# Memory updates moved behind PV as 32-column matmuls, maxima transposed by VectorE, a finer head

## The chip, the cores and the metric

The kernel runs on one core of a Trainium2 chip. The metric is the device time of one execution in microseconds (us); the median of three runs before the change is 1011.85 us. A core has five engines with a queue each, executed in order: TensorE (PE in the profile, its weight loads as PEld), VectorE (DVE), ScalarE (ACT), GpSimd (POOL) and SyncE (SP, which issues all DMAs here). They meet through semaphores.

## What is computed

Two attention branches, A and B, over the same x (2048 tokens of 640 features, 32 heads of 20), mixed per token by a gate. Each branch goes through four segments of 512 tokens and carries a memory `M`, `z` per head:

```python
def _A_ref(x, wq, wk, wv, wo, beta):
    # q, k, v: x @ w, split into 32 heads and 4 segments of 512 tokens
    phi = lambda t: jnp.where(t > 0, t + 1.0, jnp.exp(t))
    for s in range(4):
        qs, ks, vs = q[:, :, s], k[:, :, s], v[:, :, s]
        logits = jnp.einsum("bhqd,bhkd->bhqk", qs, ks) * scale + mask
        a_dot = jnp.einsum("bhqk,bhkd->bhqd", _softmax(logits), vs)
        pq = phi(qs)
        num = jnp.einsum("bhld,bhde->bhle", pq, M)
        den = jnp.einsum("bhld,bhd->bhl", pq, z)[..., None] + 1e-6
        outs.append(g * num / den + (1.0 - g) * a_dot)      # g = sigmoid(beta)
        pk = phi(ks)
        M = M + jnp.einsum("bhld,bhle->bhde", pk, vs)
        z = z + jnp.einsum("bhld->bhd", pk)
    return o @ wo                                            # o: outs put together

g = _sigmoid((x * gate_w).sum(-1, keepdims=True))
return g * A(x) + (1 - g) * B(x)
```

The mask lets a query see keys up to its own position in the segment.

## The kernel before

The work is cut into eight windows t = 2 x segment + branch. Features are tiled in five blocks m of 128 (a block touches 7 or 8 heads), tokens in four blocks n of 128. The projections run at full precision as three products of high and low parts (`wh`, `wl` of the weights, rows `hi`, `lo` of x). High and low parts of q and k go to DRAM (`qd`, `kd`) and come back by groups of four heads, a "quad" i = 8t + u, into `qst[i % 4]`, `kst[i % 4]`, with two heads on partitions 0 to 63 and two on 64 to 127.

Each quad then takes these steps:

- S units (`s_unit`, L1236 on PE): scores with queries on the partitions. DVE takes the row maxima (L1223) into `mx`.
- The maxima are split in high and low (`m_unit`, `mt`, one tile of 128 x 32), transposed and written into the spare rows of `qst` by two DMAs. Before the change the transpose is `mrow_unit`: two turns on PE (L1261), a cast on ACT to `mr` (L1278).
- T units (`t_unit`, L1326): scores again with keys on the partitions, the maximum subtracted by those rows, exp on ACT, the triangle cut by POOL.
- PV (`pv_unit`, L1346): the sums over keys, four heads side by side, each with 32 columns of weights from `vst` (v and a column of ones, 21 columns a head), over all 128 rows of the array.

The memory of a branch is `mbds[t % 2][m]`: for each feature of block m, its sums with the 21 columns of each head the block touches. `got_pk` turns phi(k) to tokens on partitions (`back_unit`, into the row `pkn`), `update_unit` (L987) multiplies it with `vst`, DVE copies the sum out, and POOL clears what belongs to other heads and adds (`keep_own_heads`, L369, L373, L1008). Windows 0 to 5 do this, five updates each. The memory after window t is read by `mem_unit` (L905) of window t + 2, which runs per token block for a lower and an upper group of heads.

Nearly all of this runs as two streams on PE: one uses the array's upper 64 rows, one the lower, and a "unit" has first a part on one half and then on the other. PV and the head use all rows at once. The order of everything is set by a planner in the kernel: it advances a clock with assumed durations, keeps the pools of SBUF rows (`big`, 35), PSUM banks (8) and weight buffers (`wst`, 3), starts queued work by priority, and has a table `RULES` with, for each quad, the order of S and T units and seven numbers (pacing, lag, room and waits). `later` puts a unit in a list that the streams draw from. `lat=` in `dma` is the time the planner assumes until a transfer has landed. The chip itself follows only the queues and semaphores that come out.

The head (`job_head`, L841) is the first two projections, while x and the first weights land. `warm_up` runs nine products of zeros ahead of it (L349), and `IDLE_STEPS` puts seven more between its steps. `head_gates` makes the sigmoids of beta (L619, L620).

## Time and profile before

| | before |
|---|---|
| three runs | 1010.74, 1011.85, 1012.91 us |
| span of the profiled execution, first to last instruction | 1010.0 us |
| granted TensorE clock | 1.000 |
| PE / PEld busy | 99% / 85% |
| DVE / ACT / POOL busy | 74% / 66% / 60% |
| DMA | 236.42 MB, mean 234 GB/s |

The profiled execution shows its span, 1010.0 us; the fastest run is 0.7 us above that and the median 1.85 us, which is the time around the instructions. Groups give the number of instructions, busy time, the mean length of one and the engine's idle time before them with what ended it; matmuls overlap, so that mean is longer than the time an instruction keeps its half of the array. A full fp32 matmul is one row of the program's order and two instructions (passes) in the profile. In a timeline, rows are start, length, engine and line, and the bracket is the idle time before.

### The profile page before, as it was taken

What the parts mean: (1) busy time and instruction counts of PE and PEld (TensorE: products, weight loads), DVE (VectorE), ACT (ScalarE), POOL (GpSimd) and SP (SyncE); (2) the same over time, 40 slices, a digit from 0 to 9 for tenths busy, and PEclk for the clock granted to TensorE, in tenths of its full rate; (3) what the DMA queues carried; (4) which work ended last, traced back from release to release, by engine and by line L of the source; (5) the groups of instructions that cost most, each with busy time, mean ns of one, the idle gap of its engine ahead of it and who ended that gap; (6) DMA issues with size and microseconds to landing.
All of it is one profiled execution on the core that took longest, in us unless ns stands there. A gap on an engine that the chain in (4) does not pass through costs nothing.

```text
span 1010.0 us, 30764 instructions
## 1 busy us (share of the span) xinstructions
PE 998.5 (99%) x11262; PEld 857.8 (85%) x11262; DVE 751.3 (74%) x2562; ACT 666.4 (66%) x1371; POOL 602.4 (60%) x1039
## 2 busy tenths in 40 slices
PE   9999999999999999999999999999999999999998
PEld 7998888978898888888889988888888897889776
DVE  4577677857897777786778857778676887789854
ACT  5476767767766677676676557766666575675682
POOL 4555657755575655666656466576675566556561
PEclk9999999999999999999999999999999999999999
DMA  7997879969796877896679677788666978658521
GB/s 241 282 313 238 284 249 317 296 197 280 241 307 211 268 224 213 255 274 204 180 227 289 196 230 229 215 273 277 200 198 201 304 235 248 201 190 269 155 89 63
DMA packets 146449, 236.42 MB, mean 234 GB/s; under 512 B 12950, under 2 KB 45883, under 8 KB 145979
## 3 DMA queue, kind: packets, MB, share of 16 engines
q1 hardware_dynamic: 146298, 234.46, 75.5%
q8 instruction: 89, 1.46, 0.6%
q14 instruction: 62, 0.50, 0.2%
HBM read 145.26 MB, written 94.65 MB: 238 GB/s over the span
## 4 chain that ended last, share of the span: by engine, by line
PE 91%; DMA 5%; DVE 2%; ACT 1%; issue 1%; SPq 0%; POOL 0%; DVEq 0%; ACTq 0%; POOLq 0%
PE bank L795 53%; PE bank L1346 14%; PE bank L1326 7%; PE bank L1236 7%; PE bank L905 3%; PE bank L987 3%; PE bank L947 2%; DMA wst<-in_a_wv_dram 1%; DMA row<-rowg 1%; PE bank L1261 1%; DMA qd<-row 1%; DMA row<-in_xT_dram 1%; DVE row L1411 1%; DMA dots<-row 1%; PE bank L1165 0%
## 5 line engine op out<-in xcount | busy, mean ns | idle before, releaser
L1223 DVE CUSTOM_DVE_ANT_0 bank<-bank,tri 128x256 f32<-128x256 f32 (+3 forms) x1024 | 474.5, 519 | 163.0 <-PE bank L1236 125.0
L795 PE MATMUL bank<-row,wh 64*128 64x512 f32 x2308 | 513.2, 402 | 0.0
L1318 ACT ACTIVATE p<-bank 128x512 f32<-128x512 f32 x548 | 301.5, 600 | 115.2 <-PE bank L1326 91.8
L795 PEld LDWEIGHTS bank<-row,wh 64*128 64x128 f32 x2308 | 329.1, 185 | 10.1 <-issue 0.2
L1319 POOL TENSOR_SCALAR_AFFINE_SELECT p<-p 128x256 f32<-128x256 f32 (+1 forms) x548 | 205.1, 382 | 200.6 <-ACT p L1318 187.1
L795 PE MATMUL bank<-row,wl 64*128 64x512 f32 x1154 | 312.5, 399 | 0.0
L549 POOL TENSOR_TENSOR wl<-wst,wh 128x640 fp32r<-128x640 f32 x115 | 180.1, 1569 | 72.7 <-ACT wh L547 69.5
L795 PE MATMUL bank<-wvh,row 64*128 64x320 f32 (+1 forms) x1280 | 191.0, 313 | 0.0
L795 PEld LDWEIGHTS bank<-row,wl 64*128 64x128 f32 x1154 | 182.9, 185 | 3.8
L1236 PE MATMUL bank<-kst,qst 60*128 60x384 f32 (+3 forms) x1024 | 177.1, 317 | 3.5 <-ACT mr L1278 2.0
L1326 PE MATMUL bank<-qst,kst 62*128 62x128 f32 (+3 forms) x1024 | 175.9, 317 | 1.3 <-DVE mx L1223 1.3
L795 PEld LDWEIGHTS bank<-wvh,row 64*128 64x128 f32 x1280 | 160.0, 185 | 2.1 <-issue 0.4
L1223 DVE DVE_READ_ACCUMULATOR2_ANT mx<- 128x1 f32 x1024 | 143.8, 140 | 0.0
L1346 PE MATMUL bank<-p,vst 128*32 128x384 f32 (+3 forms) x1836 | 141.4, 423 | 0.0
L1236 PEld LDWEIGHTS bank<-kst,qst 60*128 60x128 f32 x1024 | 132.6, 186 | 9.5 <-ACT mr L1278 2.8
L1326 PEld LDWEIGHTS bank<-qst,kst 62*128 62x128 f32 x1024 | 130.7, 186 | 6.8 <-DVE mx L1223 2.4
L1346 PEld LDWEIGHTS bank<-p,vst 128*32 128x32 f32 x1836 | 57.4, 110 | 80.9 <-issue 58.2
L795 PE MATMUL bank<-wvl,row 64*128 64x320 f32 (+1 forms) x640 | 109.1, 312 | 0.0
L547 ACT CAST wh<-wst 128x640 fp32r<-128x640 f32 x119 | 86.7, 740 | 25.1 <-PE bank L795 17.7
L795 PEld LDWEIGHTS bank<-wvl,row 64*128 64x128 f32 x640 | 87.0, 186 | 0.4 <-issue 0.2
L1376 ACT COPY row<-bank 128x512 f32<-128x512 f32 x58 | 34.2, 590 | 69.8 <-PE bank L1346 64.9
L524 POOL TENSOR_TENSOR wvl<-wst,wvh 128x640 fp32r<-128x640 f32 (+1 forms) x48 | 60.1, 1258 | 31.9 <-ACT wvh L521 30.9
(121 smaller groups left out, 1223.4 us busy)
## 6 DMA issues: line engine op xcount, KB each, us to landing
qst<-qd SPq DMA_DIRECT2D x128, 240.0 KB
kst<-kd SPq DMA_DIRECT2D x128, 240.0 KB
qd<-row SPq DMA_DIRECT2D x40, 512.0 KB
kd<-row SPq DMA_DIRECT2D x40, 512.0 KB
dots<-row SPq DMA_DIRECT2D x56, 256.0 KB
wst<-wmix SPq DMA_DIRECT2D x35, 320.0 KB
row<-dots SPq DMA_DIRECT2D x42, 256.0 KB
qd<-row SPq DMA_DIRECT2D x40, 256.0 KB
```

Source lines behind the costliest of these rows:

```text
L524: put("G", 0.77 * n, lambda: nc.gpsimd.tensor_tensor(out=wl[:, a:b, :VN], in0=w3, in1=r32(wh[:, a:b, :VN]), op=ALU.subtract), end, prio=4)
L547: put("A", 0.625, lambda: nc.scalar.copy(wh, w3), lambda: put(lo_eng, lo_cost, lambda: lo.tensor_tensor(out=wl, in0=w3, in1=r32(wh), op=AL ...
L549: lambda: lo.tensor_tensor(out=wl, in0=w3, in1=r32(wh), op=ALU.subtract), end, prio=3), prio=6)
L795: return nc.tensor.matmul(bank_of, lhsT=w[ROWS[half]], rhs=x_[ROWS[half]], start=start, stop=stop)
L905: return nc.tensor.matmul(pm[:, a - h0:c - h0, :].rearrange("p h e -> p (h e)"), lhsT=r32(pqTs[t, m][ROWS[half], P * n:P * (n + 1)]), rhs= ...
L1223: put("D", w / 960.0 + 0.105, lambda: nc.vector.tensor_tensor_reduce(out=sc[:, off:off + w], in0=sc[:, off:off + w], in1=tri[:, L - w:], s ...
L1236: lane_ops[half].append((mm(w), lambda pair=pair, qb=qb, off=off, w=w, r=r, sc=sc: nc.tensor.matmul(sc[:, off:off + w], lhsT=q[r, pair, P ...
L1318: put("A", 0.483, lambda: nc.scalar.activation(pt, sc, AF.Exp, scale=SCALE), lambda: (bank.give(sc), put("G", 0.15 + 0.105 * len(todo), la ...
L1319: "G", 0.15 + 0.105 * len(todo), lambda: nc.gpsimd.affine_select(out=blocks, in_=blocks, pattern=[[0, len(todo)], [1, P]], base=0, channel ...
L1326: lane_ops[half].append((mm(w), lambda pair=pair, kb=kb, off=off, w=w, r=r, sc=sc: nc.tensor.matmul(sc[:, off:off + w], lhsT=k[r, pair, P ...
L1346: nc.tensor.matmul(po[32 * j:32 * j + 32, P * kb:], lhsT=vst[t % 2][:, kb, h * E1:h * E1 + 32], rhs=pts[i, n, f][0][:, off:off + w], start ...
L1376: either(0.483, lambda: nc.scalar.copy(r32(oT), po), 0.605, lambda: nc.vector.tensor_copy(r32(oT), po), end, 2)
```

## The change

Six things change together.

1. `update_unit` goes. An update now waits in `upd_due` until the next PV, behind whose matmuls up to three run (`updates`), with 32 features as weights over all 128 rows and only the 2 or 3 heads these touch as columns. One update is 16 matmuls in four column groups instead of 8 matmuls on halves. The result is copied by four DVE copies of 32 partitions; memory and `mt` tiles are zeroed at the start, since each copy writes only its window. The v products of window t + 2 wait for the update's matmuls, not for the whole update.
2. `mrow_unit` goes: DVE transposes the maxima, four blocks of 32 x 32 (`turn_rows`), straight into `mr`.
3. The head runs single products as soon as their parts are there; the seven idle steps go. x of the first segment is staged through four rows, and weights beyond the first two are asked for once the first x tile has been split.
4. Memory units are split at head 16 instead of 19.
5. The planner assumes longer landing times for wv (1.2 to 2.6), later x (1.2 to 3.0) and the gate rows and denominators (1.2 to 2.2).
6. `RULES` is another table, with an entry for every quad.

```diff
-        0: "STTSTSSTST 1.010 2.38 0.25 8 0.0 1.6 1",
...
+        0: "TSTSTSTSTS 1.01 2.38 0.23 8 0 1.6 1",
+        1: "SSTSTSTSTT 1.01 2.38 0.34 8 1.4 1.6 1",
...
-    IDLE_STEPS = {3: 5, 4: 2}
...
+        for t in (*mbds[0], *mbds[1], *mt_store.free):
+            nc.gpsimd.memset(t, 0.0)
...
-        if i >= len(jobs) or i in staged:
+        if i >= len(jobs) or i in staged or i >= len(HEAD0) and not x_begun:
...
-                dma(0.53 * n, lambda: nc.sync.dma_start(out=w3, in_=src[m // 4][:, a:b, :]), landed, prio=need[i], lat=1.2)
+                dma(0.53 * n, lambda: nc.sync.dma_start(out=w3, in_=src[m // 4][:, a:b, :]), landed, prio=need[i], lat=2.6)
...
+    x_first = Store([])
+    x_first_rows, x_begun = [], []
...
+                x_hi[s, k] = (hi, lo)
...
+                if s:
+                    big.give(st)
+                    return
+                x_first.give(st, *([x_first_rows[-1]] if k == 0 else []))
+                if k == 0:
+                    x_begun.append(1)
+                    for i in range(len(HEAD0), 9):
+                        stage(i)
+                if k == KT - 1:
+                    big.give(*x_first_rows)
...
-                out=r32(st), in_=xT[P * k:P * (k + 1), L * s:L * (s + 1)]), landed, prio=need[job_index[2 * s, "q", 0]] - 4 * (s > 0), lat=1.2 if s else 1.1)
-
-        big.want((F32R, F32R, F32), got, prio=4, spare=SPARE if s else 0)
+                out=r32(st), in_=xT[P * k:P * (k + 1), L * s:L * (s + 1)]), landed, prio=need[job_index[2 * s, "q", 0]] - 4 * (s > 0), lat=3.0 if s else 1.1)
+
+        if s:
+            big.want((F32R, F32R, F32), got, prio=4, spare=SPARE)
+        else:
+            x_first.want(1, lambda st: big.want((F32R, F32R), lambda hi, lo: got(hi, lo, st), prio=4))
...
-        todo = [(k, i) for k in range(KT) for i in range(len(HEAD0))]
+        todo = [(k, i, j) for k in range(KT) for i in range(len(HEAD0)) for j in range(3)]
         pps, n = {}, {}
+
+        def there(x):
+            k, i, j = x
+            return i in (split if j == 1 else split_hi_) and (0, k) in (xs if j == 2 else x_hi)
+
         while todo:
-            ready_ = [x for x in todo if x[1] in split and (0, x[0]) in xs]
-            if not ready_:
+            x = next((x for x in todo if there(x)), None)
+            if x is None:
                 blocked[0] = "head"
                 yield None
                 continue
-            k, i = ready_[0]
-            todo.remove((k, i))
+            todo.remove(x)
+            k, i, j = x
             if i not in pps:
                 pps[i], n[i] = bank.free.pop(0), 0
-            (wh, wl), (xh, xl) = split[i], xs[0, k]
-            for w, x_ in ((wh, xh), (wl, xh), (wh, xl)):
-                whole(STEP, lambda: nc.tensor.matmul(
-                    pps[i], lhsT=w[:, k, :], rhs=x_, start=(n[i] == 0), stop=(n[i] == 3 * KT - 1)))
-                n[i] += 1
-
-                for _ in range(IDLE_STEPS.get(sum(n.values()), 0)):
-                    idle_step()
-                yield STEP
+            w, o = split_hi_[i][j == 1], x_hi[0, k][j == 2]
+            whole(STEP, lambda: nc.tensor.matmul(
+                pps[i], lhsT=w[:, k, :], rhs=o, start=(n[i] == 0), stop=(n[i] == 3 * KT - 1)))
+            n[i] += 1
+            yield STEP
...
-        h0, h1 = ((0, 19), (19, 32))[h]
+        h0, h1 = ((0, 16), (16, 32))[h]
...
-                later(3, 1.0, lambda: ok(), lambda: update_unit(t, m, pkn), False)
+                upd_due.append((t, m, pkn, ok))
...
-    def update_unit(t, m, pkn):
+    upd_due = deque()
+    upd_run = set()
+    UPD = 63 / 1200.0 + 0.0027
+
+    def windows(m):
+        for j in range(4):
+            f0 = P * m + 32 * j
+            a, c = f0 // DH, (f0 + 31) // DH + 1
+            yield slice(32 * j, 32 * j + 32), a, c
+
+    def updates():
+        todo = [x for x in upd_due if x[3]()][:3]
+        if not todo or not bank.free:
+            return
+        b = bank.free.pop(0)
+        off = 0
+        done = then_all(len(todo), lambda: bank.give(b))
+        for x in todo:
+            upd_due.remove(x)
+            t, m, pkn, _ = x
+            nh = HI[m] - LO[m] + 1
+            v = b[:, off:off + nh * E1].rearrange("p (h e) -> p h e", e=E1)
+            off += nh * E1
+            for n in range(NB):
+                for r, a, c in windows(m):
+                    nc.tensor.matmul(
+                        v[r, a - LO[m]:c - LO[m], :].rearrange("p h e -> p (h e)"),
+                        lhsT=r32(pkn[:, P * n + r.start:P * n + r.stop]), rhs=vst[t % 2][:, n, a * E1:c * E1],
+                        start=(n == 0), stop=(n == NB - 1), skip_group_check=True,
+                    )
+            now[0] += 8 * UPD
+            upd_run.add((t, m))
+            after_whole(lambda t=t, m=m, pkn=pkn, v=v: updated(t, m, pkn, v, done))
+        advance(now[0])
+
+    def updated(t, m, pkn, v, done):
         s = t // 2
-        mbd = mbds[t % 2]
+        mbd = mbds[t % 2][m]
         nh = HI[m] - LO[m] + 1
-        b = bank.free.pop(0)
-
-        def run(half, n, start, stop):
-            return nc.tensor.matmul(
-                b[:, :nh * E1], lhsT=r32(pkn[ROWS[half], P * n:P * (n + 1)]),
-                rhs=vst[t % 2][ROWS[half], n, LO[m] * E1:(HI[m] + 1) * E1],
-                start=start, stop=stop,
-            )
-
-        ops = [[(quad4(nh * E1), lambda a, z, half=half, n=n: run(half, n, a, z)) for n in range(NB)] for half in range(2)]
-        v = b[:, :nh * E1].rearrange("p (h e) -> p h e", e=E1)
 
         def end():
             upd_done.add((t, m))
 
...
-        return split_unit(*ops, take)
+        def take(dst):
+            for r, a, c in windows(m):
+                h = slice(a - LO[m], c - LO[m])
+                nc.vector.tensor_copy(dst[r, h, :], v[r, h, :])
+
+        def got(tmp):
+            def add():
+                keep_own_heads(tmp[:, :nh, :], m)
+                nc.gpsimd.tensor_tensor(out=mbd, in0=mbd, in1=tmp[:, :nh, :], op=ALU.add)
+
+            put("D", 0.44, lambda: take(tmp), lambda: (
+                done(), put("G", 1.34, add, lambda: (mt_store.give(tmp), end()), prio=2)), prio=3)
+
+        big.give(pkn)
+        if s == 0:
+            put("D", 0.44, lambda: take(mbd), lambda: (
+                done(), put("G", 0.8, lambda: keep_own_heads(mbd, m), end, prio=2)), prio=3)
+        else:
+            mt_store.want(1, got)
...
-        yield from hold_on(lambda: t < 2 or oTs_begun[t - 2] == 8 and all((t - 2, m) in upd_done for m in range(KT)), "v")
+        yield from hold_on(lambda: t < 2 or oTs_begun[t - 2] == 8 and all((t - 2, m) in upd_run for m in range(KT)), "v")
...
     def m_ready(i):
         m_done.add(i)
-        later(0, 0.2, lambda: True, lambda: mrow_unit(i))
-
-    def mrow_unit(i):
+        mr_store.want(1, lambda mr: put("D", 0.4, lambda: turn_rows(i, mr), lambda: send_rows(i, mr), prio=1), prio=0)
+
+    def turn_rows(i, mr):
+        mt = mts.pop(i).rearrange("p f c n -> p (f c n)")
+        for j in range(NB):
+            nc.vector.transpose(r32(mr[:, 32 * j:32 * j + 32]), r32(mt[32 * j:32 * j + 32, :]))
+
+    def send_rows(i, mr):
         t, u, q, k = quad(i)
-        mt = mts.pop(i)
-        b = bank.free.pop(0)
-        mtf = r32(mt.rearrange("p f c n -> p (f c n)"))
-        ops = [[(TURN, lambda a, z, r=r: nc.tensor.transpose(b[:32, r], mtf[r], ident[r, r]))] for r in ROWS]
-
...
-            put("A", 0.15, lambda: nc.scalar.copy(mr, b[:32, :P]), send, prio=1)
-
-        return split_unit(*ops, lambda: mr_store.want(1, got))
+
+        def sent():
+            mr_done.add(i)
+            mr_store.give(mr)
+
+        done = then_all(2, sent)
+        for half in range(2):
+            r = 64 * half + 60
+            dma(0.3, lambda half=half, r=r: nc.sync.dma_start(
+                out=r32(q[r:r + 2, :, :].rearrange("p a (b n) -> p (a b) n", b=NB)),
+                in_=r32(mr[16 * half:16 * half + 16, :]),
+            ), done, prio=-2, some=True, issue=0.68)
...
             advance(now[0])
+        updates()
         now[0] += 0.11
...
-            out=r32(d), in_=lanes_of(t)[:, DH:DH + 1, :].to_broadcast([H, 4, L])), landed, prio=-1, lat=1.2)
+            out=r32(d), in_=lanes_of(t)[:, DH:DH + 1, :].to_broadcast([H, 4, L])), landed, prio=-1, lat=2.2)
...
-    put("G", 1.6, ones_tiles, prio=1)
+    put("G", 2.8, ones_tiles, prio=1)
+    big.want((F32,) * 4, lambda *rows: (x_first_rows.extend(rows), x_first.give(*rows[:3])))
     for k in range(KT):
         if k < len(HEAD0):
             stage(k)
         want_x(0, k)
-    for i in range(len(HEAD0), 9):
-        stage(i)
```

Three places show how the order moves. First PE in window 0, where the update of one feature block stands (`bank<-vst,row`); before, the rows of an update lie between those of the projections:

```order
L795 MATMUL bank_139<-row_25_199,wh_145 128x512
L795 MATMUL bank_137<-row_15_193,wh_147 128x512
L795 MATMUL bank_139<-row_30_202,wh_145 128x512
L795 MATMUL bank_137<-row_20_196,wh_147 128x512
L987 MATMUL bank_135<-vst_88,row_229_369 128x147
L795 MATMUL bank_137<-row_25_199,wh_147 128x512
L987 MATMUL bank_135<-vst_88,row_229_369 128x147
L795 MATMUL bank_139<-row_7_189,wh_145 128x512
L987 MATMUL bank_135<-vst_88,row_229_369 128x147
L1236 MATMUL bank_134<-kst_84,qst_80 128x512
```

and after, behind the last block of PV (L1392) of quad 0:

```order
L1392 MATMUL bank_137<-p_890_998,vst_88 32x256
L1392 MATMUL bank_137<-p_781_915,vst_88 32x128
L1392 MATMUL bank_137<-p_782_916,vst_88 32x128
L1392 MATMUL bank_137<-p_843_966,vst_88 32x128
L1392 MATMUL bank_137<-p_844_967,vst_88 32x128
L1031 MATMUL bank_136<-vst_88,row_223_369 32x42
L1031 MATMUL bank_136<-vst_88,row_223_369 32x63
L1031 MATMUL bank_136<-vst_88,row_223_369 32x42
```

The eight half-height rows of 147 columns have left the two streams, and the update stands in one piece behind PV, 42 and 63 columns wide.

Second, the maxima of quad 0 (`mt`). Before, PE turns them between projections:

```order
L987 MATMUL bank_140<-vst_88,row_351_551 128x147
L795 MATMUL bank_138<-row_19_195,wh_151 128x512
L678 MATMUL bank_134<-ident,gate 32x64
L1261 MATMUL bank_141<-ident,mt_676 32x64
L795 MATMUL bank_136<-row_7_189,wh_149 128x512
L795 MATMUL bank_138<-row_24_198,wh_151 128x512
L795 MATMUL bank_136<-row_14_192,wh_149 128x512
```

and after, DVE turns them between the maxima (L1275, where "ISA" is the custom maximum and its read-out into `mx`) of later quads and the low parts of projections (L786):

```order
L1275 ISA bank_135,mx_545<-bank_135,tri 128x128
L1275 ISA mx_545 128x1
L645 TENSOR_SCALAR gate<-gate 128x4 x2
L1311 STREAM_TRANSPOSE mr_160<-mt_668 32x32 x4
L786 TENSOR_TENSOR row_514_695<-bank_139,row_513_694 128x512
L1275 ISA bank_140,mx_716<-bank_140,tri 128x512
L1275 ISA mx_716 128x1
L786 TENSOR_TENSOR row_520_701<-bank_136,row_519_700 128x512
L1275 ISA bank_134,mx_716<-bank_134,tri 128x512
```

The turn has left PE and stands on DVE, four transposes in a row.

Third, ACT in the head. Before, the high parts of x (`row<-row`) follow each other, and the sigmoids of beta (`gmem`, `gdot`, `gcol`) come behind them and two weights:

```order
L592 CAST row_14_192<-row_16_194 128x512
L592 CAST row_19_195<-row_21_197 128x512
L592 CAST row_24_198<-row_26_200 128x512
L592 CAST row_29_201<-row_31_203 128x512
L547 CAST wh_149<-wst_144 128x640
L547 CAST wh_151<-wst_142 128x640
L521 CAST wvh<-wst_143 128x2x320
L619 ACTIVATE gmem_92<-beta_204 128x32
L619 ACTIVATE gdot_94<-beta_204 128x32
```

and after:

```order
L604 CAST row_20_195<-row_5_189 128x512
L604 CAST row_25_197<-row_6_190 128x512
L644 ACTIVATE gmem_92<-beta_199 128x32
L644 ACTIVATE gdot_94<-beta_199 128x32
L644 ACTIVATE gcol_132<-gcol_132 128x1
L644 ACTIVATE gmem_93<-beta_200 128x32
L644 ACTIVATE gdot_95<-beta_200 128x32
L644 ACTIVATE gcol_133<-gcol_133 128x1
L604 CAST row_72_233<-row_4_188 128x512
L604 CAST row_77_236<-row_7_191 128x512
```

The six activations on beta now stand between the third and the fourth x tile.

42 lines of the change are left out of this document (8 added, 34 removed), and 122 rows, old and new, of the table RULES.

## The prediction

> **What bounds the kernel now.** I read the page's busy table and its chain first, then the waits of TensorE, then the groups kept apart by shape, then the timeline at the places the change touches.
>
> ```profile
> span 1010.0 us, 30764 instructions
> PE 998.5 (99%) x11262; PEld 857.8 (85%) x11262; DVE 751.3 (74%) x2562; ACT 666.4 (66%) x1371; POOL 602.4 (60%) x1039
> PE 91%; DMA 5%; DVE 2%; ACT 1%; issue 1%; SPq 0%; POOL 0%; DVEq 0%; ACTq 0%; POOLq 0%
> ...
> PE bank L1236 <- ACT mr L1278: 2.0, 2, 1.5
> ...
> PE bank L1326 <- DVE mx L1223: 1.3, 1, 1.3
> ...
> PE bank L947 <- DVE row L751: 0.4, 1, 0.4
> ...
> PEld bank L1346 <- issue: 63.5, 256, 0.4
> PEld bank L1261 <- issue: 7.3, 37, 0.2
> ```
>
> PE busy at 99% alone would prove little, since matmul ends are modelled. The waits prove more: the six rows of the matmul queue's waits for other engines, first and last shown, sum to 6.7 us (1.5 of them at the very start), the chain is 91% PE, and most work runs as two independent streams, one on each half of the array's rows. So a microsecond of array time that is removed is a microsecond of span, as long as the other engines keep up. An instruction on one half counts half. The few real stalls come from in-order queues:
>
> ```profile
> 218.20 0.72 ACT L521 CAST wvh<-wst 128x640 fp32r<-128x640 f32 x1 [2.16 <-DMA wst<-in_a_wv_dram]
> 218.83 0.25 ACT L1278 CAST mr<-bank 32x128 fp32r<-32x128 f32 x1
> 219.13 0.50 PE L1236 MATMUL bank<-kst,qst 60*128 60x512 f32 x1 [1.45 <-ACT mr L1278]
> ...
> 423.43 0.44 PE L1326 MATMUL bank<-qst,kst 62*128 62x384 f32 x2 [1.34 <-DVE mx L1223]
> ...
> L1406 DVE SCALAR_TENSOR_TENSOR row<-row,gcol,row 128x512 f32<-128x512 f32 x7 | 7.6, 1079 | 6.4 <-DMA row<-rowg 6.3
> ```
>
> ACT stands 2.16 us in front of a weight that has not landed, the small `mr` cast is queued behind it, and PE loses 1.45 us. At 423 us the same happens on DVE behind the gate rows (L1406).
>
> **The updates.** The trace has 480 passes of L987 (a full fp32 matmul is two), 240 on each half.
>
> ```profile
> L987 PE MATMUL bank<-vst,row 64*128 64x147 f32 x384 | 50.0, 288 | 0.0
> L987 PE MATMUL bank<-vst,row 64*128 64x168 f32 x96 | 17.9, 310 | 0.0
> ...
> 212.22 0.28 PE L987 MATMUL bank<-vst,row 64*128 64x147 f32 x1
> 212.34 0.41 PE L987 MATMUL bank<-vst,row 64*128 64x147 f32 x2
> ```
>
> One pass lasts 0.28 us and two in a row 0.41, so a 147-column pass occupies its half for 0.125-0.13 us (0.125 from here on), a 168-column one by ratio 0.143. Removed: (384 x 0.125 + 96 x 0.143) / 2 = 30.9 us of the array.
>
> What comes instead, 16 matmuls per update with 32-column weights over all 128 rows, has one relative in the trace, PV:
>
> ```profile
> L1346 PE MATMUL bank<-p,vst 128*32 128x256 f32 x512 | 39.4, 379 | 0.0
> L1346 PE MATMUL bank<-p,vst 128*32 128x128 f32 x484 | 25.2, 273 | 0.0
> L1346 PEld LDWEIGHTS bank<-p,vst 128*32 128x32 f32 x1836 | 57.4, 110 | 80.9 <-issue 58.2
> ...
> 68.14 2.36 PE L1346 MATMUL bank<-p,vst 128*32 128x512 f32 x32
> ...
> 68.13 0.16 PEld L1346 LDWEIGHTS bank<-p,vst 128*32 128x32 f32 x8 [0.19 <-issue]
> 68.59 0.13 PEld L1346 LDWEIGHTS bank<-p,vst 128*32 128x32 f32 x4 [0.30 <-issue]
> ```
>
> Four column groups stream side by side. 128 columns more cost 379 - 273 = 106 ns, 0.83 ns a column. A window of 32 features touches 2 or 3 heads, 42 or 63 columns, so by streaming a pass of the four groups takes 63 x 0.83 + 3 = 0.055 us; an update is 4 blocks x 2 passes = 8 of them, 0.44 us, and 30 updates 13.2 us. The bounds: if the 42-column groups set the pace (0.035), 8.4 us; if each pass had to wait out a whole load (0.110 us), 26.4 us. No row has a stream this short, and PV's last block (128 columns, 106 ns) is as long as its load, so it cannot decide. I take 13.2, because eight loads of 0.11 us fit in 0.16 us: they start 7 ns apart, so the loads of four groups overlap instead of queueing, and four are issued at 68.59 while the stream before them runs on. Net -17.7 us (between -4.5 and -22.5). The drain of the array around PV is paid already, since the updates sit directly behind it.
>
> [...]
>
> Each update also waits for the next PV (64 in 1010 us, so up to 16 us) holding one of 35 SBUF rows. Nobody reads the memory before the window two steps on; I cost that at nothing, and if rows run short the T units wait.
>
> **The maxima.** 128 transposes on PE (L1261) and 64 ACT casts go; 256 transposes of 32x32 come to DVE.
>
> ```profile
> 213.97 0.40 PE L795 MATMUL bank<-row,wh 64*128 64x512 f32 x1
> ...
> 214.71 0.22 PE L1261 MATMUL bank<-ident,mt 64*32 64x64 f32 x1
> 214.74 0.47 PE L795 MATMUL bank<-row,wl 64*128 64x512 f32 x1
> ...
> L921 DVE RECIPROCAL mw<-mw 128x13 f32<-128x13 f32 x24 | 5.8, 241 | 0.8
> L919 DVE SCALAR_TENSOR_TENSOR mw<-bank,gq 128x13 f32<-128x13 f32 x24 | 4.0, 165 | 2.1 <-PE bank L905 2.1
> L1010 DVE COPY mt<-bank 128x147 f32<-128x147 f32 x16 | 4.7, 302 | 3.1 <-PE bank L987 3.1
> ...
> 275.00:400.00 125.00, 125.00 (x1443) 109.05 (x1440) 100.10 (x327) 82.42 (x168) 78.70 (x135) 1.00 0.80 245
> ```
>
> A turn takes 0.03 us of its half, and the product behind it starts some 0.08 late (0.47 against 0.40), since its weights cannot load earlier: 0.11 us. In 37 of 128 cases (the issue waits above) a turn comes straight behind PV, where the array is refilling anyway; those are free. (128 - 37) x 0.11 / 2 = -5.0 us (between 0 and -7).
>
> DVE has no such transpose in the trace. By its smallest operations it costs 0.165 to 0.241 us, 42 to 62 us for 256. The copies of an update become four of 32 partitions: 120 x 0.165-0.3 less 30 x 0.302, 11 to 27 us more. DVE goes from 751 to some 805-840 us of 984, and in its densest stretch, 275 to 400 us (third busy figure of that row), from 100 in 125 to about 109 in 122. It has room, but queues lengthen: I add 2.5 us of PE waits, 0.04 us for each of the 64 quads (between 0 and 12). ACT loses 64 x 0.25 us, worth nothing.
>
> **Memory units.** Split at 16, the lower unit needs one matmul less per token block:
>
> ```profile
> L905 PE MATMUL bank<-mbd,row 64*128 64x21 f32 x48 | 8.1, 247 | 0.0
> ...
> 697.68 4.81 PE L905 MATMUL bank<-mbd,row 64*128 64x84 f32 x74
> ```
>
> 74 passes in 4.81 us over both halves are 0.062 each whatever their width, so 48 fewer are -3.0 us (0 to -3).
>
> **The head.**
>
> ```profile
> 1.52 4.21 PE L349 MATMUL bank<-qst 128*128 128x512 f32 x9 [1.52 <-DVE qst L353]
> ...
> 5.52 0.78 PE L841 MATMUL bank<-row,wh 128*128 128x512 f32 x1
> 6.69 1.31 PE L349 MATMUL bank<-qst 128*128 128x512 f32 x5
> ...
> 8.29 2.70 ACT L592 CAST row<-row 128x512 fp32r<-128x512 f32 x4 [1.78 <-DMA row<-in_xT_dram]
> ...
> 13.48 0.23 ACT L619 ACTIVATE gmem<-beta 128x32 f32<-128x32 f32 x1
> ...
> 14.70 0.39 PE L841 MATMUL bank<-row,wh 128*128 128x512 f32 x1
> ...
> 16.17 0.20 ACT L619 ACTIVATE gcol<-gcol 128x1 f32<-128x1 f32 x1 [0.35 <-DVE gcol L626]
> ```
>
> 30 steps of about 0.23 us are 7.0, but the head runs from 5.52 to 14.9, so 2.4 us are fillers and waiting for x. Fewer transfers in flight and finer steps should recover that. Against it, the six beta activations, which took 13.48 to 16.37 with DVE in between, now stand on ACT ahead of the last two x casts, and x tile 3 is sent only when tile 0's row is free. I take -1.2 (0 to -2.4). Without fillers PE may idle about 1 us at a time. The rows of L349 show full rate by then: five in 1.31 us, where the first nine took 4.21. [...]
>
> **The assumed landing times** (wv, x, gate rows) are raised, which moves the instruction that stalled at 218 us behind other work. PE's waits behind such places are the 6.7 us above less the 1.5 at the start, about 5; I take -3.5 (0 to -5). The new table of rules may move as much either way.
>
> **Sum.** -17.7 - 5.0 - 3.0 - 1.2 - 3.5 + 2.5 = -27.9 us, a span of 982.1 against 1010.0. The median of the runs, 1011.85, is 1.85 above that span; with the same offset, 984.
>
> **Rivals.**
> 1. The short passes are paced by their loads: 26.4 instead of 13.2, so 997. For it: no stream under 106 ns in the trace. Against it: the loads 7 ns apart. 11%.
> 2. Loads do not overlap at all: 0.055 + 0.110 a pass, 30 x 8 x 0.165 = 39.6 us, more than the 30.9 removed, so 984 + 26.4 = 1010, no change. PV's 2.36 us speaks against it. 3%.
> 3. DVE becomes the bound: it must come out slower if more than 28 us of the 53-89 us added to DVE surface on PE, 0.44 us a quad. The stall at 423 us shows the path (maxima late, S units keep their banks, PE waits); against it stand DVE's 259 idle us, 4 a quad. It would give about 1015. 4%.
> 4. The other stalls go too, another 8 us: 976. 14%.
>
> The forecast as told, 977 to 991, has 68%. The range from 973 to 997 takes in rivals 1 and 4 in the main and leaves out 2 and 3. By the three runs (1010.74 to 1012.91) a change under 0.2%, 2 us, cannot be told from none: faster 0.93, same 0.03, slower 0.04.
>
> **What would show it.** Right: L987 and L1261 gone; the 32 short matmul passes behind a PV within about 0.45 us; turns on DVE under 0.25 us; the waits of PE on ACT `mr` gone; the head ending near 13.7 us; DVE near 82%. Wrong: updates near 0.9 us each; PE waiting for DVE's maxima or transposes; T units waiting for SBUF rows.

## The result and the profile after

| | before | after |
|---|---|---|
| median of the runs shown together | 1011.45 us (1010.74 to 1012.91) | 997.84 us (997.83 to 999.21) |
| span of the profiled execution | 1010.0 us | 996.1 us |

The ratio is 0.9875, with a 95% interval from 0.9856 to 0.9894. The forecast was 984 with a range from 973 to 997: the direction was right, the gain was half of what was told (13.6 us instead of 27.9), and the time lies just above the range.

First the page of the changed kernel: span, busy times, and the shares of the chain.

```profile
span 996.1 us, 31535 instructions
...
PE 979.4 (98%) x11559; PEld 821.2 (82%) x11559; DVE 814.0 (82%) x2904; ACT 654.4 (66%) x1310; POOL 604.5 (61%) x1052
...
PE 84%; DVE 7%; DMA 4%; issue 2%; POOL 2%; SPq 1%; ACT 1%; DVEq 0%; ACTq 0%; POOLq 0%
```

PE is as busy as before, and DVE is at the 82% that was forecast. The chain has changed: DVE carried 2% of it, some 20 us, and now carries 7%, some 70 us. PE's share fell from 91% to 84%. Something on DVE now ends last.

The new work, in the groups kept apart by shape (line 1031 is the updates, 1052 their copies, 1311 the turned maxima):

```profile
L1311 DVE STREAM_TRANSPOSE mr<-mt 32x32 f32<-32x32 f32 x256 | 51.0, 199 | 26.9 <-POOL mt L1300 24.2
...
L1031 PE MATMUL bank<-vst,row 128*32 128x63 f32 x384 | 14.0, 219 | 0.0
...
L1031 PE MATMUL bank<-vst,row 128*32 128x42 f32 x576 | 13.3, 204 | 0.0
L1052 DVE COPY mt<-bank 32x42 f32<-32x42 f32 x48 | 9.5, 197 | 4.6 <-PE bank L1031 2.3 <-issue 1.2
...
L1052 DVE COPY mt<-bank 32x63 f32<-32x63 f32 x32 | 7.0, 219 | 3.8 <-PE bank L1031 2.5 <-POOL mbd L1057 0.7
...
L1052 DVE COPY mbd<-bank 32x42 f32<-32x42 f32 x24 | 4.8, 198 | 3.5 <-PE bank L1031 3.1
L1052 DVE COPY mbd<-bank 32x63 f32<-32x63 f32 x16 | 3.5, 219 | 3.6 <-PE bank L1031 3.4
```

And the timeline of PE at two updates behind a PV:

```profile
64.77 0.62 PE L1392 MATMUL bank<-p,vst 128*32 128x256 f32 x12
65.20 0.97 PE L1031 MATMUL bank<-vst,row 128*32 128x42 f32 x64
```

Sixty-four passes (two updates) end within 0.97 us, and one pass lasts 0.20 to 0.22, so 64 of them start within 0.76 us, 12 ns apart. An update takes 32 x 12 ns = 0.39 us of the array, and 30 take 11.7. That is a little better than the 13.2 of the prediction. The 64 weight loads of these passes, 0.11 us each and 7.0 in sum, run within 0.92 us, from 65.10 to 66.01. In the kernel before, of the 2.36 us of PV's 32 passes at 68.14 the streams took 2.12 (2 x 1280 columns x 0.83 ns), so eight loads of 0.11 us one after the other had no room there either. The two rivals about weight loads are out. A copy takes about 0.2 us, four for an update 0.83, and a turn of four transposes 0.8.

Now the waits of the matmul queue for other engines (total us, times, longest):

```profile
PE bank L1288 <- DVE mt L1052: 2.8, 3, 1.2
PE bank L1288 <- DVE mbd L1052: 2.8, 3, 1.7
PE bank L356 <- DVE qst L360: 1.5, 1, 1.5
...
PE bank L1372 <- DVE mt L1052: 0.9, 2, 0.5
...
PE bank L1372 <- DVE mbd L1052: 0.6, 1, 0.6
```

The wait on ACT's `mr` (2.0 us before) is gone, as forecast. In its place stand the copies: 2.8 + 2.8 + 0.9 + 0.6 = 7.1 us in which no matmul ran at all. A half of the array that stands while the other half works isn't in this list, so the whole price is larger. The weight-load queue (PEld) has a list of its own, and it is longer. Its rows that name DVE sum to 29.4 us here and to 9.7 in the kernel before; 10.3 of the 29.4 name the copies and 9.4 the maxima, which had 4.5 before. The first three of these rows:

```profile
PEld bank L1372 <- DVE mx L1275: 3.9, 13, 0.6
PEld bank L1288 <- DVE mbd L1052: 3.9, 3, 2.1
PEld bank L1288 <- DVE mt L1052: 3.6, 3, 1.7
```

The largest place shows the mechanism. DVE first, then PE, in the timeline of the changed kernel:

```profile
93.84 2.67 DVE L1052 COPY mbd<-bank 32x63 f32<-32x63 f32 x12 [3.38 <-PE bank L1031]
96.54 0.70 DVE L1275 CUSTOM_DVE_ANT_0 bank<-bank,tri 128x512 f32<-128x512 f32 x1
```

```profile
92.40 1.36 PE L1031 MATMUL bank<-vst,row 128*32 128x63 f32 x96
93.69 0.50 PE L1288 MATMUL bank<-kst,qst 60*128 60x512 f32 x2
94.02 0.85 PE L820 MATMUL bank<-row,wl 64*128 64x512 f32 x5
96.56 0.50 PE L1288 MATMUL bank<-kst,qst 60*128 60x384 f32 x4 [1.69 <-DVE mbd L1052]
```

DVE stands 3.38 us in front of the first copy, since the three updates (96 passes) end on PE only then. Then the copies of three updates run in one burst, twelve in 2.67 us, until 96.51. The S unit that PE starts at 96.56 begins while the maximum behind the burst (L1275, 96.54 to 97.24) still runs, so it wasn't waiting for a maximum. By the kernel's code it can only want a bank that the copies have emptied: `updates` takes one bank for the sums of up to three updates, and gives it back when all of them are copied. The planner assumes 0.44 us for the copies of an update, 1.3 for three, and has laid the unit into that bank too early. PE has nothing to do for 1.69 us. The row maxima, whose scores have lain in their banks since 94.2, are late as well; they show in the rows of the weight-load queue.

### The profile page after: what moved, and what is told of

The parts are those of the page before. It is cut to its first block, busy times and chain, and to the rows that moved or that the text cites. A ratio compares the mean times of both kernels' runs of the same rounds, so it can differ in the third digit from the quotient of the medians.

```text
span 996.1 us, 31535 instructions
## 1 busy us (share of the span) xinstructions
PE 979.4 (98%) x11559; PEld 821.2 (82%) x11559; DVE 814.0 (82%) x2904; ACT 654.4 (66%) x1310; POOL 604.5 (61%) x1052
## 3 DMA queue, kind: packets, MB, share of 16 engines
q8 instruction: 91, 1.49, 0.6%
## 4 chain that ended last, share of the span: by engine, by line
PE 84%; DVE 7%; DMA 4%; issue 2%; POOL 2%; SPq 1%; ACT 1%; DVEq 0%; ACTq 0%; POOLq 0%
PE bank L820 51%; PE bank L1392 13%; PE bank L1288 7%; PE bank L1372 7%; PE bank L973 2%; PE bank L931 2%; DMA row<-dots 1%; DVE mt L1052 1%; DVE bank L1275 1%; DVE mbd L1052 1%; PE bank L1031 1%; DMA row<-rowg 1%; DMA dots<-row 1%; DMA kd<-row 1%; DVE mr L1311 1%
## 5 line engine op out<-in xcount | busy, mean ns | idle before, releaser
L1275 DVE CUSTOM_DVE_ANT_0 bank<-bank,tri 128x384 f32<-128x384 f32 (+3 forms) x1024 | 474.4, 520 | 86.6 <-PE bank L1288 75.0
L820 PE MATMUL bank<-row,wh 64*128 64x512 f32 x2308 | 479.7, 402 | 0.2
L1364 ACT ACTIVATE p<-bank 128x512 f32<-128x512 f32 x550 | 301.5, 605 | 141.5 <-PE bank L1372 113.4
L820 PEld LDWEIGHTS bank<-row,wh 64*128 64x128 f32 x2308 | 308.6, 185 | 16.8 <-PE bank L820 1.8
L1365 POOL TENSOR_SCALAR_AFFINE_SELECT p<-p 128x128 f32<-128x128 f32 (+1 forms) x550 | 203.4, 378 | 188.3 <-ACT p L1364 171.6
L820 PE MATMUL bank<-row,wl 64*128 64x512 f32 x1154 | 292.7, 398 | 0.0
L820 PEld LDWEIGHTS bank<-row,wl 64*128 64x128 f32 x1154 | 172.2, 185 | 7.7 <-issue 1.0
L820 PE MATMUL bank<-wvh,row 64*128 64x320 f32 (+1 forms) x1280 | 166.0, 312 | 0.6 <-DVE row L770 0.6
L1275 DVE DVE_READ_ACCUMULATOR2_ANT mx<- 128x1 f32 x1024 | 144.4, 141 | 0.2
L1288 PEld LDWEIGHTS bank<-kst,qst 60*128 60x128 f32 x1024 | 128.3, 185 | 18.6 <-DVE mbd L1052 3.9
L820 PEld LDWEIGHTS bank<-wvh,row 64*128 64x128 f32 x1280 | 140.7, 185 | 3.1 <-DVE row L770 0.9
L1392 PE MATMUL bank<-p,vst 128*32 128x384 f32 (+3 forms) x1840 | 141.8, 423 | 0.0
L1392 PEld LDWEIGHTS bank<-p,vst 128*32 128x32 f32 x1840 | 57.4, 110 | 82.2 <-issue 58.7
L820 PE MATMUL bank<-wvl,row 64*128 64x320 f32 (+1 forms) x640 | 99.4, 311 | 0.0
L1311 DVE STREAM_TRANSPOSE mr<-mt 32x32 f32<-32x32 f32 x256 | 51.0, 199 | 26.9 <-POOL mt L1300 24.2
```

The source lines that it names most:

```text
L820: return nc.tensor.matmul(bank_of, lhsT=w[ROWS[half]], rhs=x_[ROWS[half]], start=start, stop=stop)
L1275: put("D", w / 960.0 + 0.105, lambda: nc.vector.tensor_tensor_reduce(out=sc[:, off:off + w], in0=sc[:, off:off + w], in1=tri[:, L - w:], s ...
L1288: lane_ops[half].append((mm(w), lambda pair=pair, qb=qb, off=off, w=w, r=r, sc=sc: nc.tensor.matmul(sc[:, off:off + w], lhsT=q[r, pair, P ...
L1311: nc.vector.transpose(r32(mr[:, 32 * j:32 * j + 32]), r32(mt[32 * j:32 * j + 32, :]))
L1364: put("A", 0.483, lambda: nc.scalar.activation(pt, sc, AF.Exp, scale=SCALE), lambda: (bank.give(sc), put("G", 0.15 + 0.105 * len(todo), la ...
L1365: "G", 0.15 + 0.105 * len(todo), lambda: nc.gpsimd.affine_select(out=blocks, in_=blocks, pattern=[[0, len(todo)], [1, P]], base=0, channel ...
```

## The experiments

The names: "the copies" are L1052, "the turns" L1311. Gains and losses in us are differences of ratios to the kernel before times 1010 us.

**One copy for each update.** The theory is that the bursts of small copies in front of the maxima ate the gain.

```diff
-            for r, a, c in windows(m):
-                h = slice(a - LO[m], c - LO[m])
-                nc.vector.tensor_copy(dst[r, h, :], v[r, h, :])
+            nc.vector.tensor_copy(dst[:, :nh, :], v)
```

> The result of an update is copied by one DVE copy of 128 partitions instead of four of 32; all else, the planner's costs included, stays, so the order of every engine is the same but for 90 copies that are gone. Copies theory (the four copies, 0.21 us each, stand in bursts of 8 to 12 in DVE's queue ahead of the maxima, S units keep their banks and PE waits): the waits of PE for L1052, 7.1 us on the matmul queue, mostly go; 6 to 9 us faster than the changed kernel, 989 to 992. Order theory (the new table and landing times make the waits, whatever DVE does): within 2 us of 998. Array theory (turns and memory units were worth less than priced, waits do not matter): within 2 us of 998.

Measured: 984.28 us (983.55 to 985.86), ratio 0.9744 [0.9719, 0.9770], 13.2 us less than the changed kernel and more than the 6 to 9 expected. From its page the busy times and the chain, then a group, the first waits of the matmul queue, and the same place in the timeline of DVE:

```profile
PE 974.3 (99%) x11559; PEld 822.3 (84%) x11559; DVE 795.4 (81%) x2814; ACT 654.1 (66%) x1310; POOL 602.7 (61%) x1052
...
PE 90%; DMA 3%; DVE 2%; POOL 2%; ACT 1%; SPq 1%; issue 1%; DVEq 0%; ACTq 0%
```

```profile
L1050 DVE COPY mt<-bank 128x147 f32<-128x147 f32 x16 | 4.4, 300 | 6.8 <-PE bank L1031 3.0 <-POOL mbd L1055 2.4 <-issue 1.2
```

```profile
PE bank L356 <- DVE qst L360: 1.5, 1, 1.5
PE bank L1286 <- DVE row L776: 1.1, 1, 1.1
```

```profile
92.85 0.77 DVE L1050 COPY mbd<-bank 128x168 f32<-128x168 f32 x3 [3.39 <-PE bank L1031]
93.53 0.69 DVE L1273 CUSTOM_DVE_ANT_0 bank<-bank,tri 128x512 f32<-128x512 f32 x1
```

DVE still stands 3.39 us in front of the updates, but three copies of 0.30 take 0.77 us instead of 2.67. The maxima follow 3 us earlier, of which this kernel was ahead by 1 us before. No wait of the matmul queue names a copy any more, and the longest but the one at the start is 1.1 us. The weight-load queue's rows that name DVE fall from 29.4 to 16.8 us, 12.6 less, which is nearly the whole gain. DVE has 18.6 us less to do (814.0 to 795.4), and its share of the chain is back at 2%. Copying the columns of other heads too costs nothing here, since POOL clears them anyway. That the time is that of the forecast, 984, is partly chance: the turns still cost more than was forecast, and other terms made up for them.

**The copies twice.** The counterpart, each copy made a second time.

```diff
+            for _ in range(2):
                 for r, a, c in windows(m):
```

> Each of the 120 copies of an update is made twice in a row, order otherwise unchanged: 25 us more of DVE. Copies theory: the bursts double in length, PE waits behind nearly every one; 10 to 20 us slower than the changed kernel, 1008 to 1018. Order and array theories: DVE has 180 idle us, so under 4 us slower.

Measured: 1041.47 us (1036.83 to 1044.26), ratio 1.0304 [1.0264, 1.0344], 43 us slower than the changed kernel, for 24.8 us more of copies (the sum of their four groups above). It is more than twice the 10 to 20 expected. The waits of PE, the timeline at one of them, and a window that begins in it (length, then PE, PEld, DVE, ACT and POOL busy, the granted clock, and the share and GB/s of the DMA engines):

```profile
PE bank L1289 <- DVE mt L1053: 11.1, 4, 4.1
PE bank L1289 <- DVE mbd L1053: 10.8, 3, 4.7
PE bank L1373 <- DVE mt L1053: 6.2, 3, 2.5
PE bank L1373 <- DVE mbd L1053: 2.6, 1, 2.6
```

```profile
474.53 0.79 PE L1373 MATMUL bank<-qst,kst 62*128 62x512 f32 x1 [2.41 <-DVE mt L1053]
```

```profile
473.90:480.70 6.80, 6.17 (x33) 5.38 (x35) 4.37 (x18) 1.72 (x3) 3.00 (x10) 0.50 0.11 37
```

The rows that name the copies come to 30.7 us, 23.6 more than in the changed kernel, about as much as the added copies take. A second price comes with them: 1.8 us into the wait of 2.41 us the granted clock falls to one half and stays there for 6.8 us. Over the whole run the mean clock was 0.982; if it was one half wherever it wasn't full, as here, that is an estimated 37 us at half rate, which lose at most 19 us of work. The two together, 23.6 and 19, come to the 43 measured.

**The turns twice.** The rival is that DVE as a whole is too full, wherever the work stands.

```diff
-        for j in range(NB):
+        for j in [*range(NB), *range(NB)]:
             nc.vector.transpose(r32(mr[:, 32 * j:32 * j + 32]), ...)
```

> Each of the 256 DVE transposes of the maxima is made twice, order otherwise unchanged: 51 us more of DVE, spread in pieces of 0.8 us over 64 quads. Copies theory (it is the burst, not the load): slower, but less per us of DVE than the doubled copies, 3 to 12 us, 1001 to 1010. If DVE's load as a whole is the bound: 15 to 30 us slower. Order and array theories: under 4 us slower.

Measured: 1031.85 us (1028.59 to 1034.35), ratio 1.0211 [1.0179, 1.0244], 34 us slower for 51 us of DVE (256 x 0.199). That is far more than the 3 to 12 us expected, and above the 15 to 30 told for DVE's load as the bound. Here the first of PE's waits names the maxima, which stand behind the turns:

```profile
PE bank L1372 <- DVE mx L1275: 4.9, 8, 1.2
```

The mean clock of 0.995 takes at most 5 of the 34 us. Without the clock's part a microsecond of the turns costs about 0.6 us and one of the copies about 1.0.

**Three of four transposes left out**, in the kernel with one copy. The maxima of three quarters of a quad's queries are then zero, since the `mr` tiles are zeroed at the start.

```diff
-        for j in range(NB):
+        for j in range(1):
             nc.vector.transpose(...)
```

> The kernel with one copy per update, and three of the four DVE transposes of each quad left out (three quarters of the maxima stay zero, so the output is not the reference's): 38 us less of DVE, order unchanged. If the DVE's load still costs PE waits: 5 to 15 us faster than 984. If the turns are hidden once the bursts of copies are gone: within 3 us of 984.

Measured: 977.87 us (977.63 to 978.38), ratio 0.9675 [0.9661, 0.9690], 7.0 us less. So the turns aren't hidden. That takes 192 x 0.199 = 38 us from DVE, so a microsecond taken from the turns gives 0.18 us; one taken from the copies gave 13.2 / 18.6 = 0.7. What a microsecond of DVE costs depends on where it stands. The turns were taken second, though, from a DVE that already had less to do, so these runs don't separate how much of the difference is due to the place alone.

**The turns alone, in the kernel before.** PE's turns aren't issued; DVE's transposes stand where ACT's cast stood in the plan.

```diff
-        ops = [[(TURN, lambda a, z, r=r: nc.tensor.transpose(b[:32, r], mtf[r], ident[r, r]))] for r in ROWS]
+        ops = [[(TURN, lambda a, z: None)] for r in ROWS]
...
-            put("A", 0.15, lambda: nc.scalar.copy(mr, b[:32, :P]), send, prio=1)
+            put("A", 0.15, lambda: turn_rows(mr), send, prio=1)
```

> The kernel before with one part of the change alone: the maxima are turned by four DVE transposes where the ACT cast stood, and PE's 128 turns are not issued; the planner's costs are those of before, so the rest of the order is the same. If a turn costs PE what the prediction priced (5.0 us in all) and DVE's room hides the 51 us added: 4 to 6 us faster than before, 1004. If DVE work that the planner does not know of comes out on PE, as the doubled turns showed (34 us for 51): 10 to 30 us slower than before.

Measured: 1032.18 us (1030.23 to 1032.50), ratio 1.0205 [1.0185, 1.0226], 21 us slower. The waits of PE:

```profile
PE bank L1236 <- DVE mx L1223: 3.9, 10, 0.7
PE bank L1330 <- DVE mx L1223: 1.7, 5, 0.6
```

S units now have ten small waits for the maxima where before they had none, and T units five where there was one (1.3 us, in the prediction's lines). The rows of the weight-load queue that name DVE rise from 9.7 to 30.9 us, by as much as the time. The step that was to bring 5.0 us costs 21 in an order that wasn't laid out for it. What it brings in an order laid out for it, no run shows.

**A quarter of the updates, in the kernel before.** This tests the prediction's first step, that array time removed is span removed. Only the last of the four token blocks of each update is multiplied, so the memories hold a quarter of the keys; by the prediction's price that is 23 us less for the array, and nothing else moves.

```diff
         def run(half, n, start, stop):
+            if n < NB - 1:
+                return None
+            start = not stop
```

> The kernel before with only the last of the four token blocks of each update multiplied (three quarters of L987 left out, so the memory is not the reference's); the order is otherwise unchanged. If the array bounds the kernel as the prediction's first step says, 0.75 x 30.9 = 23 us go: 986 to 990. If waits for other engines fill what is freed: less than 10 us faster, above 1000.

Measured: 1011.09 us (1007.85 to 1018.10), ratio 1.0013 [0.9991, 1.0035]. No change. The first rows of PE's waits:

```profile
PE bank L1239 <- ACT p L1321: 2.5, 2, 1.3
...
PE bank L1239 <- ACT mr L1281: 1.4, 3, 0.6
PE bank L1329 <- DVE mt L1013: 1.1, 1, 1.1
```

PE waits more for ACT and DVE, whose work stands where the old lengths had put it. But that is only a part. All rows of the matmul queue sum to 10.9 us instead of 6.7, and those of the weight-load queue to 120.3 instead of 108.5, so some 11 of the 23 us are in no row. Most of the time doesn't show even on the spot. Of the 480 passes, 240 stand before the maximum of the two lines below; the three quarters of these that are left out are worth 11.6 us by the prediction's price. The same maximum starts only 2.9 us earlier (first line before, second line this run):

```profile
331.61 0.70 DVE L1223 CUSTOM_DVE_ANT_0 bank<-bank,tri 128x512 f32<-128x512 f32 x1 [0.46 <-PE bank L795]
```

```profile
328.69 0.70 DVE L1226 CUSTOM_DVE_ANT_0 bank<-bank,tri 128x512 f32<-128x512 f32 x1 [0.45 <-PE bank L795]
```

A cause may be, by the author's estimate, that the passes of an update use one half of the array at a time and stand in PE's queue between products on the other half, whose length stays. That they count half for the span whatever the other half does was the prediction's assumption. No run tests this by itself.

**The updates twice, in the kernel before.** The opposite: each update matmul is issued a second time, into unused columns.

```diff
+            for o in (256, 0):
+                r = nc.tensor.matmul(
+                    b[:, o:o + nh * E1], ...
```

> The kernel before, with each matmul of an update run twice, the first time into unused columns of its bank; nothing else moves. It adds 480 passes, by the prediction's price 30.9 us of the array. The counterpart, three quarters of the update passes left out, changed nothing (ratio 1.0013). If the array's time paces the kernel only upwards, since the order was laid out for just this much work, the added time counts nearly in full: 1035 to 1042. If the other queues pace it with room to spare on the array, little of it shows: 1010 to 1020. If the prediction's price of a pass is too high, the time lies in proportion below 1041.

Measured: 1052.56 us (1051.62 to 1054.82), ratio 1.0410 [1.0385, 1.0436]: 41 us for 30.9 by the prediction's price. With the run before: in this order, passes added count in full and more, and passes removed count nothing. That fits an order laid out for just these lengths, and it fits passes that stand on one half beside work on the other; the two runs don't tell these apart.

**A quarter of the updates, in the kernel with one copy.** The memories hold a quarter of the keys again; 8.8 us less for the array.

```diff
-            for n in range(NB):
+            for n in range(NB - 1, NB):
...
-                        start=(n == 0), stop=(n == NB - 1), skip_group_check=True,
+                        start=True, stop=True, skip_group_check=True,
```

> The kernel with one copy for each update (984.28 us), in which an update multiplies only the last of its four token blocks, so the memories hold a quarter of the keys; everything else stands in the same order. By the profile of the changed kernel this takes 8.8 us of array time away. If array time that is removed becomes span in this order, 975.5. If an order that is laid out for given lengths doesn't pass a saving on, as in the kernel before (ratio 1.0013 for 23 us less), 983 to 985.

Measured: 978.93 us (978.55 to 980.73), ratio 0.9692 [0.9673, 0.9710], 5.3 us less. Here some 60% of the removed time becomes span; by the two intervals it can be 2 to 8.5 us of the 8.8. What is removed here used all rows of the array, and in the kernel before one half at a time, so the difference between the two runs needn't come from the order.

**The updates twice, in the kernel with one copy.**

```diff
-            for n in range(NB):
+            for n in [*range(NB)] * 2:
```

> The kernel with one copy for each update (984.28 us), with the 16 short matmuls of each of the 30 updates run twice, the second time from a fresh start; everything else stands in the same order. By the profile of the changed kernel the updates cost 11.7 us of the array in all. If the array's time paces the kernel, the time is 984.3 + 11.7 = 996. If the order of the other queues paces it, as the run with a quarter of the updates says, part of it or all stays hidden: 984 to 990.

Measured: 1025.94 us (1022.38 to 1031.15), ratio 1.0149 [1.0119, 1.0180], 41 us slower for 11.7 of array time, which neither theory had. The waits of PE, and the timeline at the longest:

```profile
PE bank L1031 <- issue: 21.4, 8, 4.8
```

```profile
597.86 2.33 PE L1031 MATMUL bank<-vst,row 128*32 128x42 f32 x171
605.01 0.85 PE L1031 MATMUL bank<-vst,row 128*32 128x42 f32 x21 [4.82 <-issue]
```

In the middle of a run of 192 short passes PE stops for 4.82 us, waiting for nothing that the profile shows. There are eight such stops, 21.4 us. The mean clock was 0.989, by the same estimate some 22 us at half rate or at most 11 us of work. With the 11.7 that makes 44, about what was measured; the order's pacing can't be read from this run. The changed kernel, whose runs are at most half as long, has no such row among the waits of its matmul queue.

What went on around the stops is in the DMA records of the trace. The page has two DMA queues that it marks as instruction. One of them in this run (packets, MB, share):

```profile
q8 instruction: 99, 1.62, 0.7%
```

That is 16 KB a packet, and one packet for 253 of the 25038 instructions of PE and PEld; in the changed kernel it is one for 254 (91 packets, 1.49 MB, for 23118). From this the author's estimate is that the queue brings PE's own instructions. A run of 192 passes has 384 with their weight loads, more than one packet's worth. In the longest stop such a packet is under way from 602.68 to 603.78 us, and PE goes on at 605.01. At all eight stops PE goes on 1.2 to 1.5 us behind the end of such a packet. That PE had run out of instructions would fit; no run tests it by itself.

**The 48 passes of the memory units put back**, in the kernel with one copy, into unused columns.

```diff
+            if h == 1 and half == 1 and j == 0:
+                nc.tensor.matmul(pm[:, 16, :], lhsT=..., rhs=mbd[m][ROWS[half], a - LO[m], :], ...)
```

> The kernel with one copy for each update (984.28 us), with one more 21-column matmul (two passes) on the lower half of the array in each of the 24 upper memory units, which writes to unused columns; the rest of the order is the same. These are the 48 passes that the split at head 16 had taken away. By the prediction's price of the memory units this gives back 3.0 us: 987.3. By the array time that the two traces show for the memory units it gives back 0.6 to 1.4: 985 to 985.7, which can hardly be told from none.

Measured: 988.44 us (988.09 to 990.52), ratio 0.9777 [0.9754, 0.9800], 3.3 us slower. That speaks for the prediction's 3.0 rather than for about 1, but the two intervals overlap, so it is not settled. Nor is the price of an added pass surely the gain of a removed one, as the runs with more and fewer updates show.

**The sigmoids of beta behind the last x tile**, in the kernel with one copy.

```diff
                 if k == KT - 1:
+                    head_gates()
                     big.give(*x_first_rows)
...
-    betas_there = then_all(2, lambda: put("D", 0.6, head_gates, prio=6))
+    betas_there = then_all(2, lambda: put("D", 0.6, lambda: x_begun.append(2), prio=6))
```

> The kernel with one copy per update, and the sigmoids of beta issued on ACT and DVE behind the last x tile of the first segment instead of between the third and the fourth; the order is otherwise unchanged. Head theory (the in-order ACT queue costs the head what the finer steps bring): the head ends 0.5 to 1 us earlier, 983.5. If x lands too late anyway: the head ends where it did, 984.3.

Measured: 983.94 us (983.59 to 984.44), ratio 0.9735 [0.9720, 0.9750]. That can't be told from the 984.28 without it. In the traces the head's last matmul starts at 13.57 us, against 13.99 in the kernel with one copy and 14.19 in the changed kernel, whose heads are the same. So the head does seem to end some 0.4 us earlier, which is twice the difference between two equal heads. It is the fastest of the kernels here that do all the work.

**The planner told the measured lengths.** Two runs change only the costs that the planner assumes, and so the order everywhere: 0.9 for the four copies and 0.83 for a turn in the changed kernel, then 0.31 for the one copy. The figure for the copies stands in two places; one is shown.

```diff
-            put("D", 0.44, lambda: take(tmp), lambda: (
+            put("D", 0.9, lambda: take(tmp), lambda: (
...
-        mr_store.want(1, lambda mr: put("D", 0.4, lambda: turn_rows(i, mr), ...
+        mr_store.want(1, lambda mr: put("D", 0.83, lambda: turn_rows(i, mr), ...
```

> The planner is told what the trace shows for DVE: 0.9 us for the copies of an update (it assumed 0.44) and 0.83 for the four turns (0.4); the order of all engines changes accordingly. Copies theory: the waits for L1052 shrink by half or more since S units are placed behind the copies, 2 to 8 us faster, 990 to 996, if the table, which was made with the other costs, still fits. Order theory: any other order moves the time by some us either way, no fewer waits for L1052. Array theory: within 3 us of 998.

```diff
-            put("D", 0.44, lambda: take(tmp), lambda: (
+            put("D", 0.31, lambda: take(tmp), lambda: (
```

> The kernel with one copy for each update (984.28 us), whose order is still laid out for an assumed 0.44 us on DVE per update; here the planner is told 0.31, about what one copy of 128 partitions takes, so it lays out another order in many places. If a truer assumption gives a better order, 976 to 984. If the table of rules holds for the order it was found with and a changed cost scatters it, as when the copies and turns were told at their measured lengths (1061 us), the time is 988 or more.

Measured: 1061.47 us, ratio 1.0515 [1.0476, 1.0553], and 1048.33 us, ratio 1.0375 [1.0346, 1.0403]. Both are 64 us slower than the kernels they start from, though the planner knew better each time; part of that is the clock (mean 0.974 and 0.977). The rule table, with an entry for every quad, was made for the order that came out with 0.44 and 0.4, and another order gets rules meant for other moments. How good an order laid out for the true lengths could be with a table of its own wasn't tried.

**One transpose for a turn**, in the kernel with one copy, with all the work done. The turned blocks then lie on 128 partitions, and eight transfers a quad carry them to `qst` instead of two.

```diff
-        for j in range(NB):
-            nc.vector.transpose(r32(mr[:, 32 * j:32 * j + 32]), r32(mt[32 * j:32 * j + 32, :]))
+        nc.vector.transpose(r32(mr[1][:, :]), r32(mt))
...
+            dma(0.3, lambda half=half, r=r: [nc.sync.dma_start(out=..., in_=mq[j, 16 * half:16 * half + 16, :],
+            ) for j in range(NB)][-1], done, ...)
```

> The kernel with one copy for each update (984.28 us), with the maxima of a quad turned by one DVE transpose of 128x32 instead of four of 32x32, all of the work done; the order is otherwise the same. It takes about 38 us of DVE away if one such transpose is as long as a small one (0.2 us). The price: the turned blocks lie on 128 partitions, so eight small transfers a quad carry the rows to qst instead of two, 384 more on SP. If the four transposes were the second part of the DVE waits that the prediction missed, the time falls by about the 6.4 us that leaving out three of four gave: 978. If the transfers come late because SP is in the way, the T units wait and it is 985 to 1000. If the large transpose takes four times as long as a small one, nothing is gained: 984.

Measured: 1079.28 us (1073.33 to 1081.18), ratio 1.0669 [1.0642, 1.0696]. The group of the transposes and three of PE's waits:

```profile
L1309 DVE STREAM_TRANSPOSE mq<-mt 128x32 f32<-128x32 f32 x64 | 13.4, 209 | 43.0 <-POOL mt L1298 42.8
```

```profile
PE bank L1286 <- ACT p L1364: 14.6, 8, 3.2
PE bank L1286 <- DMA kst<-kd: 7.4, 4, 4.3
...
PE bank L1372 <- DMA qst<-mq: 5.3, 5, 2.1
```

The transpose did what was hoped: 0.209 us for all four blocks, against 4 x 0.199. Three more blocks on other partitions cost 0.01 us in this run. But there are 384 more transfers, of 2 KB each, on the one queue that issues all transfers. The rows (`mq`) and the quads (`kst`) come late, and PE waits longest for the exponentials of T units (L1364), which need those rows. That costs far more than the 7 us to be had. The mean clock of 0.979 takes at most 11 of the 93 us.

## Where the prediction was right and where it failed

- **Updates** (-17.7): the price of the new passes was right. They take 11.7 us of the array instead of 13.2, and the loads of the four column groups overlap (64 of 0.11 us within 0.92). Behind PV the first pass of an update starts 0.09 us after PV's last one, at all twelve places; in the kernel before, what followed PV on halves began to load its weights 0.20 us after it, at all 64. So the updates pay no drain of their own, as the prediction had it. What the 30.9 us of removed passes were worth for the span, no run shows; in the old order 23 of them gave nothing.
- **The DVE waits** (+2.5): this is the step that failed. The prediction put it as "0.04 us for each of the 64 quads (between 0 and 12)" and argued with DVE's 259 idle us. It counted the copies at 0.165 to 0.3 us each, which is what they take, but spread them over the quads. They come in bursts of up to twelve, on an in-order queue and behind a wait for PE. PE waits for the bank that they empty, which the plan gives out again after 0.44 us an update where the copies take 0.83, and for the maxima behind them. The copies cost 13.2 us (by the run with one copy) and the turns at least 7.0 (by the run that leaves three of four out of the kernel with one copy), together 20.2 instead of 2.5 and above the stated bound of 12. The weight-load queue's rows that name DVE say the same: 9.7 us before, 29.4 in the changed kernel, 16.8 with one copy, 10.7 with one transpose of four besides. From run to run the last two fall by 12.6 and 6.1 us, and the time by 13.2 and 7.0.
- **The maxima** (-5.0): the 0.199 us of a transpose lies inside the bounds, the casts and their wait are gone. That loads came late behind PE's turns is in the trace of the kernel before: behind 117 of the 128 the next weight load starts within 5 ns of the turn's own start. If the 5.0 us came, the 7 us above take them back; in the old order this part of the change loses 21.
- **Memory units** (-3.0): 3.3 by the run that puts the passes back, not settled.
- **The head** (-1.2): about -0.5. Its last matmul started at 14.70 us before and starts at 14.19 now; it was to end near 13.7. ACT waits for DVE among the six beta activations, ahead of the last x casts. The first row is ACT's, the second PE's, both from the timeline of the changed kernel:

```profile
9.97 0.20 ACT L644 ACTIVATE gcol<-gcol 128x1 f32<-128x1 f32 x1 [1.60 <-DVE gcol L651]
```

```profile
14.19 0.40 PE L870 MATMUL bank<-row,wh 128*128 128x512 f32 x1
```

- **Landing times** (-3.5): the stalls that it spoke of are gone. ACT's waits for the wv weights fell from 10.9 us to 2.0, and DVE's 6.3 us in front of the gate rows no longer appear. PE's wait for `mr` would have gone in any case, since the cast left ACT. What this part was worth isn't measured; it moves the whole order.
- **The new table**, of which the prediction said that it may move as much either way: not tried alone. The two runs with other assumed lengths lose 64 us each, more than all terms of the sum, so how well order and table fit is the largest thing left open.
- **The first step**, "a microsecond of array time that is removed is a microsecond of span": false for the old order (0 of 23 us), about 0.6 for the updates in the new one.

Put together: -30.4 for all terms but the DVE waits, as the prediction has them, plus 20.2 measured, is -10.2, against -12.6 by the ratio. The rest, some 2 us, is within what the intervals leave open. That the two are so near isn't proof of the other terms, since what the updates, the landing times and the table gave the span wasn't measured. Rival 3 (DVE becomes the bound) named the right engine. Its path, maxima late and banks held, is in the rows too, but the longest waits of the matmul queue are for the banks of the updates themselves. It asked for 28 us to surface; 20 did.
